# Window attention on one core: staged column heads, two-block stores, nine tiles moved off ScalarE, a new order and a reworked lead

## The chip, the cores and the metric

One core of one Trainium2 chip runs the kernel. The metric is device time in microseconds (us) of one execution. TensorE multiplies matrices into the eight PSUM banks, ScalarE computes exponentials, VectorE and GpSimd do elementwise work, and the SyncE queue issues most transfers. In the profile these are PE (with PEld for its weight loads), ACT, DVE, POOL and SP.

## The reference

The input x is an image of 224 x 224 positions with 96 channels. One product gives q, k and v. The first 48 channels attend inside horizontal stripes, 28 stripes of 8 rows; the other 48 inside vertical stripes, 28 of 8 columns. Each stripe has 1792 tokens. The two results stand side by side and go through the output product.

```python
qkv = jnp.einsum('bhwc,cd->bhwd', x, wqkv)
q, k, v = (qkv[..., :C].copy(), qkv[..., C:2 * C].copy(), qkv[..., 2 * C:].copy())
scale = C2 ** (-0.5)
ah = _softmax(jnp.einsum('bqc,bkc->bqk', qh, kh) * scale, axis=-1)     # horizontal stripes
oh = jnp.einsum('bqk,bkc->bqc', ah, vh).reshape(B, H, W, C2)
av = _softmax(jnp.einsum('bqc,bkc->bqk', qv, kv) * scale, axis=-1)     # vertical stripes
ov = jnp.einsum('bqk,bkc->bqc', av, vv).reshape(B, nw, H, sw, C2)
...
return jnp.einsum('bhwc,cd->bhwd', o, wo)
```

## The kernel before

Two stripes are worked together, one on partitions 0 to 63 and one on 64 to 127. Such a pair is called a block, P = 0 to 27: blocks 0 to 13 are horizontal, 14 to 27 vertical (the first and the second half in what follows). A block has four query chunks (three of 512 columns, one of 256) and 49 score tiles of 128 x 1024 values.

A score tile gets its exponential in one of two ways. An A tile: TensorE multiplies (`qk_fn`, L689) into one of two fixed pairs of PSUM banks, ScalarE takes the exponential (L859). A polynomial tile, kind P or R, leaves ScalarE alone: TensorE multiplies (`s_fn`, L702) into a pair of the four ring banks, VectorE makes a first form of it (L943, and for kind R L945 too), GpSimd squares it (P: L959, L960, L956; R: L956 alone), TensorE multiplies a second time and VectorE finishes (L948). A VectorE pass takes the 1024 columns at once (letters 3 and 4 of the order) or as two halves of 512 (letters 1 and 2). `KINDS` and `KIND_OF` say which tiles of which block are polynomial: nine in a block of kind 1, eight in a block of kind 2. Every tile ends in the product with V (L715, letter v), which gathers in one ring bank; `emit_ot` (L876) takes that out.

Beside the tiles run the fills, letter k: K, Q and V of the next block (L521, L566, brought out on VectorE by L526, L535, L573), and in the second half letter g, the output product of `out_fills` (L637, brought out by L642). Letter f is the last block's own finish, `fin_fills` (L602, L609, L614).

The sequence of TensorE is the string `ORDER`, written out: q is an A tile, 1 and 3 the first multiplication of a polynomial tile, 2 and 4 the second. While it is read, a planner with measured durations (`D_H`, `D_F`, `SEMD`, `XR1` and so on) puts the instructions of the other engines in order; its times set the order alone. Semaphores keep each dependency on the chip. Each engine and queue works strictly in its order, so one late entry holds all that stand behind it.

The array `cat` holds both heads' outputs, 96 channels of every position. `keep_oh` writes horizontal outputs into it, `emit_norm` (L920) vertical ones, `turn_cat` (L414) transposes 96-channel rows to `oc_T` for the output product, which then needs one or two matmuls per 128 tokens as the rows straddle the 128-wide transposes (`wo6` holds six shifted copies of wo). The result goes back into `cat` and out to memory, one DMA per 128 tokens of a stripe (24 KB), from `emit_evict` (issue line L287).

At the start x comes in four loads of 168 KB, two queues with two each, then the weights on SP. `t_lead` transposes x on TensorE (L737), VectorE and ScalarE bring it out and sum it (L749, L753); `KB` makes the mean key out of the sums (L759, L763), the first K goes out by L770. `spin` (L368) puts matmuls on zeros into TensorE's waits, by the planner's times. The first eleven A tiles after the first have their matmuls doubled (`NTWICE`).

Of the kernel before, what the change touches and what calls it, by code (L numbers as in the profile page):

```python
# [20 lines left out]
KINDS = ["PPR PPR PP ", "PPR PRR PPR ", "PPR PPR PR "]  # L21
# [18 lines left out]
NTWICE = 11  # L40


KIND_OF = [0, 1, 1, 1, 1, 1, 1, 1, 1, 1, 1, 1, 1, 1, 2, 2, 2, 2, 2, 2, 2, 2, 2, 2, 2, 2, 2, 2]
ORDER = [
    "kkkqkq3qkq3qkkqkq1qkqq1q3qvkqv2qvkqv2qvqkkvqv1qkvqvkqvv2qvqv1qvvvqvkq2vqvkqkq1qkvvq2qvv2qvvq1vqkvqvvq1vqv2qvkvqvkvq",
    "1vqvvqvq2vvq3qvvvqvv3qqvqvvqkkkq2qvqvkvqv2qkvqv2qkvvvq1qvvvvqvqvv1qvvq2vq2qvkqvvq1vqvkq2vqv2qvvq1qvvqvkqvvkqkvqvkq2vvq2qvv3",
    "qvvqv1qvvq1vqvvqvvqv1qkq1qvvvqvq2qvkkqvqvk2qvvq3qvkqvkvq4qkqv1qvvq4qvkq2vqv1qvq4vqkq2vqv1qvvqvvqv2q1qvvqvkkqq1vkv",
    "qv2qvqv1qvvvqvvqv1qq1vvqvvqvvvq4qvkvq1vqvvqvq2vqv1qvv4qkqvv1qvqvkq2vqkvvq2vkqvkq3vqkqvvvqv1qvq4vqkq3vqkvq4vqvkvq4vqkvq2vk",
    "qvvq1vqvvvvqq2vvvqvvvq2vqvq14qvqkqv3qvkvqvvqvkqv1qkqvvq1vqvkq2vqvkq2qvvvq1qv1qkqvvvqkqvvkq2qvv3qkvqv3qvvqv4qvkqv4qkqvv1",
    "qvqvvvq2vqq1vvqvv1qvvqvqv2qq4vqvkq1vqvvvqvq1vqkvkqkvvq2kqv3qkvqv4qvvqkq1vqvvvqkqvv4qvqkv2qvvq2vqv1qvq4vqvvqkvkvq1qkvvq2v",  # L50
# [5 lines left out]
    "qvvq1vqvvqvq1vqv2qvvq1vqqvvvq1qkvvqvvqkvq4vqkvq1vkqv2qvq3qkvvq2kqvvq2qvv1qvqvvqv2qkvqv3qvkqv4qkqvv1qvvqkkqvkvq2qvvq2vvv",  # L56
    "q3qvvvqvvvqv1qvq2vvvqkq1vqvvq3qvvvqvvqvkq4qkvq1vkqq2vqv4qvkqv2qvvvq1vkqvkq4vqkqv2qvvvq1qvkqvvvq2qkqvvq1vvq2qvvkqkvq1vkq",
    "1qvvqvvq1qvv2qqvvq1vvqvqvv1qvqvqkvqv2qvkqv2qvvqk2qvkqv3qvkvq3qvvvq4qvkvq2qkvqkvq1vqvqkvvqvvq2vqvvq3qvvkq4vqkvqv2qvvq1vk",
    "qvq1vqvvqvvqv1qvv2qvvq1vqq2vqkvq1qvkqvvqvkvqv1qkvvq2qkvvq4vqvvkq1qvvvqvvqkqv4qkvqv4qkvvq1qvvq1vvvqv1qvqvvvvq4qvvvkq2qkvvqkvq2",
    "vvvvqq1vvvvqv2qvvq4vqvkq1qkvkqgqvkgqv3qgvqvqvvgq3qvkvq4qvgqv3qvvkqvvqkqvvgq2vqv2qvvq1vqkqvvvqvq3gqvvq4vqvvkqkq4vqgvvq4qvvkqvq1k",  # L60
    "vqvvqvvq1vqggqgvq1qvgvqkvq4vqgvq2vkqkqvv2qvkqgvq3qvkvqvkqv4qvvqvkq1vqkqv4qvvvqv1qvvqvvqkvqvvq1vqvkkqvq2vvqv4qgvqvvq3qvkvqgvq",
    "gvq1vqvqvvq3vqvkq2vvqv1qvgqvkq4qvkvq4vqvgq4vqvvkq1qvvvqvvqvvkq2qvv1qkvqkvq2qvvgq3qkvqvvqvvvq1qvv2qkqgvqvkqkvqg4qvvqkvvq3vqvgq",
# [111 lines left out]
def bass_standalone__window_attn_cswin__vision_kernel(  # L174
# [28 lines left out]
    with es:  # L203
# [25 lines left out]
        cat = sb("cat", [128, NPH, NPH, 2, C], BF16)  # L229
# [86 lines left out]
        for hf in range(2):  # L316
            for w, q in ((0, "sp"), (1, "actq")):
                dma(q, [], [("x", w, hf)], x0_sb[:, w, hf * FTH:(hf + 1) * FTH, :],
                    x_lead[w][:, hf * FTH * C:(hf + 1) * FTH * C], f"x{w}{hf}", land=3.4 + 1.0 * hf + 0.3 * w)
        dma("sp", [], ["wst"], wst[:, :], wqkv, "w0", land=5.2)  # L320

        pool_now(["iota"], lambda e: e.iota(ident_f[:], [[1, 128]], base=0, channel_multiplier=-1,
                                            allow_small_or_imprecise_dtypes=True), 0.3)
        dve_now(["warm0"], lambda e: e.memset(warm[:, 0:128], 0.0), 0.1)
# [27 lines left out]
        def later():  # L352
# [6 lines left out]
            pool_now([("cat", NPH - 1)], lambda e: e.memset(cat[:, NPH - 1, :, :, C2:C].rearrange("p m w c -> p (m w) c").bitcast(FP32), 0.0), 0.7)  # L359
            pool_now(["wo6z"], lambda e: e.memset(wo6[:].rearrange("p v c -> p (v c)").bitcast(FP32), 0.0), 0.3)  # L360
# [78 lines left out]

        def turn_cat(P, z):  # L440
            b, a = P % 2, P - NPH
            k0, k1 = ((0, 8), (8, NKT))[z]
            flat = cat[:, a, :, :, :].rearrange("p m w c -> p (m w c)")
            x_old = [("x", w) for w in range(2)] if P in (NPH, NP - 1) else []
            turn(f"oc{b}{z}", ["oh", ("cat", a), ("ov", a, z)], [("ocT", b, z), ("catd", a, z)] + x_old,
# [911 lines left out]
```

## Time and profile before

| what | value |
|---|---|
| median of three runs | 1062.24 us (1061.93 to 1062.27) |
| the profiled execution | 1062.68 us, span 1060.9 us |
| granted TensorE clock, mean | 0.999 |
| busy share of the span | PE 97%, DVE 94%, ACT 99%, POOL 88% |
| A tiles (L859) | 1135, 1044.8 us busy |

The span runs from the first to the last instruction; the time of a run holds a little more. A busy share is the union of an engine's instructions. A VectorE instruction that follows another at once starts before that one has ended, so a busy DVE holds less work when packed tightly than the sum of single durations. The views of a stretch are cut at the first A tile of a block: block 1 begins at 47.80 us, block 14 at 526.68, block 15 at 565.17, block 26 at 980.68.

### The profile page before, as it was taken

The page shows a single profiled execution, that of the slowest core. Times are in us where ns is not written, and L with a number is a line of the kernel's source. Part 1 is how long each engine was busy: PE and PEld are TensorE (multiplying, and loading weights), DVE is VectorE, ACT ScalarE, POOL GpSimd, SP SyncE. Part 2 cuts the span into 40 slices and gives each one's busy share as a digit, 9 for nine tenths or more (in the row PEclk, how much of TensorE's full clock was granted, in tenths as well). Part 3 has the DMA queues.
Part 4 walks back from the last instruction along what each step waited for, and adds up shares of the span by engine and source line. Part 5 has one row for each costly group of instructions (what it writes and reads, how often), then busy time and mean ns, then how long its engine had stood idle before and what let it go on. Part 6 is the DMA issues. An engine that isn't in the chain of part 4 may idle for free.

```text
span 1060.9 us, 33547 instructions
## 1 busy us (share of the span) xinstructions
PE 1033.4 (97%) x13812; PEld 393.5 (37%) x13812; DVE 998.2 (94%) x1720; ACT 1049.3 (99%) x1146; POOL 935.5 (88%) x617
## 2 busy tenths in 40 slices
PE   9999999999999999999999999999999999999998
PEld 4333333333333333333334433333343443344433
DVE  8999999999999999999999999999999999999988
ACT  8999999999999999999999999999999999999998
POOL 7999999999988989999999778888888878979784
PEclk9999999999999999999999999999999999999999
DMA  9987648754963874322115334423332342332342
GB/s 182 160 153 112 100 80 145 112 96 84 144 96 56 139 108 69 38 56 58 40 20 99 76 54 76 88 38 77 80 69 52 81 83 49 79 79 40 64 65 44
DMA packets 376217, 88.58 MB, mean 83 GB/s; under 512 B 366944, under 2 KB 373376, under 8 KB 376064
## 3 DMA queue, kind: packets, MB, share of 16 engines
q1 hardware_dynamic: 374816, 85.85, 46.8%
q8 instruction: 108, 1.77, 0.7%
q10 hardware_dynamic: 1120, 0.49, 0.2%
q14 instruction: 45, 0.37, 0.1%
q0 software_dynamic: 128, 0.10, 0.0%
HBM read 28.36 MB, written 28.21 MB: 53 GB/s over the span
## 4 chain that ended last, share of the span: by engine, by line
PE 54%; ACT 28%; DVE 7%; issue 6%; POOL 4%; DMA 0%; ACTq 0%; POOLq 0%; DVEq 0%
ACT PT L859 28%; PE ps L715 20%; PE ps L689 20%; PE ps L702 7%; PE ps L521 3%; DVE qb L943 2%; DVE PT L948 2%; PE ps L637 2%; POOL PT L959 2%; PE ps L566 1%; POOL PT L956 1%; POOL PT L960 1%; DVE PT L945 1%; DVE KT_sb L526 1%; POOL cat L920 0%
## 5 line engine op out<-in xcount | busy, mean ns | idle before, releaser
L859 ACT ACTIVATE PT<-ps 128x1024 bf16<-128x1024 f32 x1135 | 1044.8, 1087 | 2.8 <-PE ps L689 1.8
L689 PE MATMUL ps<-QT_sb,KT_sb 49*64 49x512 bf16 (+1 forms) x5368 | 465.3, 363 | 17.6 <-ACT PT L859 10.5
L956 POOL TENSOR_TENSOR PT<-PT 128x1024 f16<-128x1024 f16 x237 | 445.1, 1892 | 41.1 <-DVE PT L945 24.1
L715 PE MATMUL ps<-PT,V_sb 128*49 128x512 bf16 (+1 forms) x3136 | 464.7, 362 | 0.3
L948 DVE SCALAR_TENSOR_TENSOR PT<-ps,PT 128x512 uint16<-128x512 f32 (+1 forms) x398 | 302.0, 787 | 20.8 <-PE ps L702 13.5
L943 DVE TENSOR_SCALAR qb<-ps 128x512 f16<-128x512 int16 (+1 forms) x404 | 302.3, 778 | 20.3 <-PE ps L702 15.8
L959 POOL TENSOR_TENSOR PT<-qb 128x1024 f16<-128x1024 f16 x141 | 266.1, 1892 | 54.8 <-DVE qb L943 24.9
L689 PEld LDWEIGHTS ps<-QT_sb,KT_sb 49*64 49x64 bf16 x5368 | 136.4, 103 | 305.8 <-ACT PT L859 280.9
L715 PEld LDWEIGHTS ps<-PT,V_sb 128*49 128x49 bf16 x3136 | 134.8, 103 | 211.1 <-issue 181.4
L702 PE MATMUL ps<-QT_sb,KT_sb 53*64 53x512 bf16 (+1 forms) x1896 | 189.4, 389 | 4.0 <-DVE PT L948 0.7
L960 POOL TENSOR_SCALAR PT<-PT 128x1024 f16<-128x1024 f16 x141 | 147.1, 1043 | 12.0
L945 DVE SCALAR_TENSOR_TENSOR PT<-ps,qb 128x512 f16<-128x512 int16 (+1 forms) x166 | 122.5, 766 | 0.5
L702 PEld LDWEIGHTS ps<-QT_sb,KT_sb 53*64 53x64 bf16 (+1 forms) x1896 | 53.8, 104 | 71.2 <-DVE PT L948 21.7
L876 DVE CAST OT_sb<-ps 113x512 bf16<-113x512 f32 x112 | 69.1, 617 | 3.0 <-PE ps L715 2.7
L535 DVE CAST QT_sb<-ps 128x512 bf16<-128x512 f32 (+1 forms) x111 | 67.2, 616 | 2.5 <-PE ps L521 1.7
L526 DVE TENSOR_SCALAR_CACHE_REDUCE KT_sb<-ps 128x512 bf16<-128x512 f32 x108 | 65.4, 616 | 1.3 <-PE ps L521 0.6
L642 DVE CAST cat<-ps 128x480 bf16<-128x480 f32 x84 | 51.5, 617 | 5.1 <-PE ps L637 4.5
L573 DVE CAST V_sb<-ps 128x480 bf16<-128x480 f32 (+1 forms) x84 | 51.7, 620 | 1.5 <-PE ps L566 1.2
L521 PE MATMUL ps<-xT_sb,w_sb 97*64 97x512 bf16 (+1 forms) x224 | 40.7, 364 | 0.0
L521 PE MATMUL ps<-xT_sb,wq_sb 97*64 97x512 bf16 x224 | 40.5, 366 | 0.1
L637 PE MATMUL ps<-wo,oc_all 128*64 128x96 bf16 x1176 | 39.9, 208 | 0.0
L566 PEld LDWEIGHTS ps<-w_sb,xT_sb 96*64 96x64 bf16 x1568 | 33.1, 112 | 17.7 <-issue 7.4
(64 smaller groups left out, 254.7 us busy)
## 6 DMA issues: line engine op xcount, KB each, us to landing
xT_sb<-xt_dram SPq DMA_DIRECT2D x28, 336.0 KB, 4.0
out_dram<-cat SPq DMA_DIRECT2D x382, 24.0 KB, 1.9
xp_dram<-in_x_dram SPq DMA_DIRECT2D x26, 336.0 KB
oc_all<-xp_dram SPq DMA_DIRECT2D x26, 336.0 KB, 4.4
xt_dram<-xT_sb SPq DMA_DIRECT2D x26, 336.0 KB, 6.4
cat<-ohn SPq DMA_DIRECT2D x52, 84.0 KB, 3.2
xt_dram<-xT_sb SPq DMA_DIRECT2D x4, 168.0 KB, 5.3
OT_tr<-OT_sb SPq DMA_TRANSPOSE x40, 3.4
```

The source lines that it names most:

```text
L521: ins = e.matmul(bk[64 * w:64 * w + 64, 0:qs], lhsT=lw, rhs=xT_sb[b][0:C + 1, w, q0:q0 + qs], start=True, stop=True)
L526: return e.tensor_scalar(KT_sb[b][:, q0:q0 + qs], bk[:, 0:qs], alpha, None, ALU.mult, ALU.add, accum_out=ksum[b][:, c:c + 1])
L689: ins = e.matmul(bank(SETS[s] + w)[64 * kh:64 * kh + 64, i * t["qs"]:(i + 1) * t["qs"]], lhsT=KT_sb[b][64 * w:64 * w + CA, kt * 128 + 64 * ...
L702: ins = e.matmul(bank(bp[w])[64 * kh:64 * kh + 64, 0:512], lhsT=KT_sb[b][64 * w:64 * w + nr, kt * 128 + 64 * kh:kt * 128 + 64 * kh + 64], ...
L715: ins = e.matmul(bank(pb)[64 * w:64 * w + CA, 0:t["qs"]], lhsT=V_sb[b][:, w, kt, :], rhs=PT[slot][:, ca:ca + t["qs"]], start=st and i == 0 ...
L859: S.commit("act", 0.0, D_ACT, None, lambda e, s=s, slot=slot: e.activation(PT[slot][:], ps[:, 512 * SETS[s]:512 * SETS[s] + 1024], ACTF.Ex ...
L943: fn, reads, writes = lambda e: e.tensor_scalar(q, l, m, a, ALU.mult, ALU.add), bk, qk
L945: fn, reads, writes = lambda e: e.scalar_tensor_tensor(y.bitcast(FP16), l, -RA * 2.0 ** 16, q, ALU.add, ALU.mult), bk + qk, ptk
L948: fn, reads, writes = lambda e: e.scalar_tensor_tensor(y.bitcast(U16), f, 128.0, y.bitcast(FP16), ALU.mult, ALU.add), bk + ptk, ptk
L956: square = ("pool", D_SQ, lambda e: e.tensor_tensor(y, y, y, ALU.mult), yk + ["pser"], yk)
L959: return [("pool", D_SQ, lambda e: e.tensor_tensor(y, q, q, ALU.mult), qk, yk), ("pool", D_AF, lambda e: e.tensor_scalar(y, y, -(QS * (RB ...
L960: ("pool", D_AF, lambda e: e.tensor_scalar(y, y, -(QS * (RB + RA) / 2) ** 2, 1.0, ALU.add, ALU.mult), yk + ["pser"], yk),
```

## The change

Seven things change together.

1. **Nine tiles.** A new kind 3, "PPR PPR PPR ", has one P tile more than kind 2 and is used for nine of the vertical blocks (15, 16, 17, 19, 20, 21, 23, 24, 25). Nine A tiles become P tiles.
2. **Staged column heads.** `cat` goes. Horizontal outputs lie in `oh_all`; for each vertical block `rows_in` copies its 48 channels into a staging tile `stg` of 128-wide rows (32 of them zero), `emit_norm` writes the vertical 48 beside them, and `turn_cat` transposes whole 128-wide rows. The output product then needs one pair of matmuls per 128 tokens, and one copy of wo. Two new POOL memsets clear `stg` at the start.
3. **Stores of two blocks of 128 tokens.** Results lie in `og`, tokens interleaved by two, and one DMA of 48 KB stores what two of 24 KB did.
4. **Pairs of fills.** A capital K or G in the order makes two fills into two adjacent banks that one VectorE instruction brings out. The order has one K and one G.
5. **Loads of the lead.** The first half of x comes in four quarter loads over both queues, the second in two loads on SP; the weights come on POOL's queue.
6. **Filler.** One spin before the second half of the transposes and one before `KB` are fixed; the two spins after the lead go. The spins in `lead_pe`, by planned times, stay.
7. **Order and planner constants** are new. Block 0 begins `kkqqkkq` in place of `kkkqkq`.

```diff
-KINDS = ["PPR PPR PP ", "PPR PRR PPR ", "PPR PPR PR "]
+KINDS = ["PPR PPR PP ", "PPR PRR PPR ", "PPR PPR PR ", "PPR PPR PPR "]
...
-KIND_OF = [0, 1, 1, 1, 1, 1, 1, 1, 1, 1, 1, 1, 1, 1, 2, 2, 2, 2, 2, 2, 2, 2, 2, 2, 2, 2, 2, 2]
+KIND_OF = [0, 1, 1, 1, 1, 1, 1, 1, 1, 1, 1, 1, 1, 1, 2, 3, 3, 3, 2, 3, 3, 3, 2, 3, 3, 3, 2, 2]
...
-        for hf in range(2):
-            for w, q in ((0, "sp"), (1, "actq")):
-                dma(q, [], [("x", w, hf)], x0_sb[:, w, hf * FTH:(hf + 1) * FTH, :],
...
-        dma("sp", [], ["wst"], wst[:, :], wqkv, "w0", land=5.2)
+        for h2, q in ((0, "sp"), (1, "actq")):
+            for w in range(2):
+                dma(q, [], [("x", w, 0, h2)], x0_sb[:, w, h2 * FQ:(h2 + 1) * FQ, :],
...
+        for w in range(2):
+            dma("sp", [], [("x", w, 1, 0), ("x", w, 1, 1)], x0_sb[:, w, FTH:2 * FTH, :],
...
+        dma("gq", [], ["wst"], wst[:, :], wqkv, "w0", land=4.6)
...
+        pool_now([("stgz", 0)], lambda e: e.memset(stg[0][:, :, :, C:].rearrange("p m w c -> p (m w) c").bitcast(FP32), 0.0), 0.5)
+        pool_now([("stgz", 1)], lambda e: e.memset(stg[1][:, :, :, :].rearrange("p m w c -> p (m w c)").bitcast(FP32), 0.0), 1.8)
...
+        def rows_in(P):
+            b = P % 2
+            dma("sp", ["oh", ("stgz", b)], [("sr", b)], stg[b][:, :, :, 0:C2].rearrange("p m w c -> p (m w) c"),
+                oh_all[:, P - NPH, :, :, :].rearrange("p m w c -> p (m w) c"), f"ri{b}")
...
-            turn(f"oc{b}{z}", ["oh", ("cat", a), ("ov", a, z)], [("ocT", b, z), ("catd", a, z)] + x_old,
+            turn(f"oc{b}{z}", [("sr", b), ("sc", b, z), ("stgz", b)], [("ocT", b, z)] + x_old,
...
-                        for i, (dq_, v) in enumerate(use):
-                            for h in range(2):
-                                ins = e.matmul(bk[64 * h:64 * h + 64, s * C:(s + 1) * C], lhsT=oc_T[b][:, q + dq_, 64 * h:64 * h + 64],
-                                               rhs=wo6[:, v, :], start=i == 0, stop=i == len(use) - 1)
+                        for h in range(2):
+                            ins = e.matmul(bk[64 * h:64 * h + 64, s * C:(s + 1) * C],
+                                           lhsT=oc_T[b][0:C, 4 * (m // 2) + 2 * h + m % 2, :].rearrange("c (t u) -> c u t", u=2)[:, u, :],
+                                           rhs=wo6[0:C, :], start=True, stop=True)
...
+        def spin1():
+            S.commit("pe", 0.0, 0.216, 0.416, lambda e: e.matmul(
+                bank(1)[0:64, 0:512], lhsT=warm[:, 0:64], rhs=warm[:, 0:512], start=True, stop=True),
+                ["warm0", "warm"], [("bank", 1)], tag=("spin",))
...
         for w, hf, bs in ((0, 0, (6, 7)), (1, 0, (2, 3)), (0, 1, (6, 7)), (1, 1, (2, 3))):
+            if (w, hf) == (0, 1):
+                spin1()
...
+        spin1()
         lead_pe(KB, 0)
...
-        spin(S.done[("dve", S.cnt["dve"] - 1)])
-        spin(S.done[("dve", S.cnt["dve"] - 1)], 128)
...
                 if ph_of(P):
-                    tm["sp"] = max(tm["sp"], st) + 1.5
+                    tm["sp"] = max(tm["sp"], st) + (2.2 if P > NPH else 1.5)
+                    if P > NPH:
+                        rows_in(P)
...
-                do_fill(c)
+                do_fill2(c.lower()) if c in "KG" else do_fill(c)
```

More of the change, by code (lines that the diff above doesn't have):

```diff
@@ L59 @@
[L59 to L62, printed above, removed]
@@ L228, in bass_standalone__window_attn_cswin__vision_kernel @@
         OT_sb = [sb(f"OT_sb{i}", [128, NTOK], BF16) for i in range(2)]
-        cat = sb("cat", [128, NPH, NPH, 2, C], BF16)
+        oh_all = sb("oh_all", [128, NPH, NPH, 2, C2], BF16)
+        stg = [sb(f"stg{i}", [128, NKT, 2, 128], BF16) for i in range(2)]
+        og = [sb(f"og{i}", [128, NKT // 2, 2, 2, C], BF16) for i in range(3)]
         OT_tr = [sb(f"OT_tr{i}", [128, NKT, 128], BF16) for i in range(2)]
@@ L883, in emit_evict, with store @@
             if len(st) > 5:
+                store(st, done)
+        def store(st, done):
+            if st:
                 for item in st[5]:
@@ L916, in fn @@
                 if ph_of(P):
[L917 removed]
+                    dst = stg[b][:, k0:k1, :, C2:C].rearrange("p m w c -> p (m w) c")
                 else:
```

215 lines of the change are left out of this document (146 added, 69 removed).

## The prediction, made before the result was known

> **What bounds the kernel now.** I read the busy line first, then the line of ScalarE's exponentials, then the stretches between block starts.
>
> ```profile
> PE 1033.4 (97%) x13812; PEld 393.5 (37%) x13812; DVE 998.2 (94%) x1720; ACT 1049.3 (99%) x1146; POOL 935.5 (88%) x617
> PE 54%; ACT 28%; DVE 7%; issue 6%; POOL 4%; DMA 0%; ACTq 0%; POOLq 0%; DVEq 0%
> ```
>
> Four engines are nearly full, and the chain of waits (second line) names TensorE before ScalarE, so neither line alone decides. The line view of the exponentials does:
>
> ```profile
> L859 ACT ACTIVATE PT<-ps x1135: 1018/1081/1276, 9.6 to 1054.9; 128x1024 bf16<-128x1024 f32 x190
>   PE ps L689: 1.8, 3
>   PEld ps L689: 280.9, 803
> ```
>
> 1135 exponentials start between 9.6 and 1054.9, one each (1054.9 - 9.6) / 1134 = 0.922 us. ScalarE waited for TensorE three times, 1.8 us in all; TensorE's tile loads waited for ScalarE 803 times. TensorE appears in the chain because it hands the banks back and forth with ScalarE, but ScalarE never rests. It is the bound. The question is who takes over when it has fewer tiles.
>
> ```profile
> core 0: us, PE busy (x) PEld busy (x) DVE busy (x) ACT busy (x) POOL busy (x), PEclk, DMA share, GB/s
> 47.80:526.68 478.88, 465.82 (x5828) 167.43 (x5824) 461.08 (x774) 478.32 (x522) 446.00 (x293) 1.00 0.58 94
> 565.17:980.68 415.51, 409.88 (x5854) 163.77 (x5850) 389.05 (x643) 415.16 (x451) 355.29 (x222) 1.00 0.35 70
> 980.68:1055.97 75.29, 74.20 (x1062) 29.52 (x1058) 67.44 (x138) 75.29 (x83) 54.86 (x37) 1.00 0.34 57
> 1055.97:1060.90 4.93, 0.69 (x12) 0.28 (x12) 2.30 (x12) 0.00 (x1) 0.68 (x2) 0.77 0.33 65
> ```
>
> First row: blocks 1 to 13, nine polynomial tiles each; DVE is busy 96.3%, POOL 93.1%, and ACT still 99.9%. So a DVE busy at 96% does not stop ScalarE. Second row: blocks 15 to 25, eight polynomial tiles and the output product each; DVE 93.6%, POOL 85.5%. All nine moved tiles fall there. The last row is the tail, 4.93 us without exponentials.
>
> **The change part by part.** *Nine tiles off ScalarE.* 9 x 0.922 = 8.3 us less, as ScalarE is the bound from 9.6 us on. What it costs elsewhere, from the line view with shapes apart:
>
> ```profile
> L943 DVE TENSOR_SCALAR qb<-ps 128x512 f16<-128x512 int16 x334 | 216.9, 684 | 12.2 <-PE ps L702 8.8
> L943 DVE TENSOR_SCALAR qb<-ps 128x1024 f16<-128x1024 int16 x70 | 85.5, 1222 | 8.1 <-PE ps L702 6.9
> L948 DVE SCALAR_TENSOR_TENSOR PT<-ps,PT 128x1024 uint16<-128x1024 f32 x76 | 92.9, 1222 | 6.0 <-PE ps L702 3.6 <-POOL PT L956 0.9 <-DVE V_sb L573 0.3
> L956 POOL TENSOR_TENSOR PT<-PT 128x1024 f16<-128x1024 f16 x237 | 445.1, 1892 | 41.1 <-DVE PT L945 24.1 <-DVE wq_sb L552 7.5 <-PE ps L715 0.7
> L959 POOL TENSOR_TENSOR PT<-qb 128x1024 f16<-128x1024 f16 x141 | 266.1, 1892 | 54.8 <-DVE qb L943 24.9 <-ACT PT L859 8.9 <-PE ps L702 7.2
> L960 POOL TENSOR_SCALAR PT<-PT 128x1024 f16<-128x1024 f16 x141 | 147.1, 1043 | 12.0
> L637 PE MATMUL ps<-wo,oc_all 128*64 128x96 bf16 x1176 | 39.9, 208 | 0.0
> 699.86 1.29 DVE L943 TENSOR_SCALAR qb<-ps 128x512 f16<-128x512 int16 x2
> 1041.93 0.46 PE L637 MATMUL ps<-wo,oc_all 128*64 128x96 bf16 x14
> ```
>
> A P tile is two DVE passes and three POOL passes. POOL: 1.892 + 1.043 + 1.892 = 4.83 us, nine times 43.4. The blocks 15 to 25 would then hold 355.3 + 43.4 = 398.7 in 415.5 - 8.3 = 407.2 us, 98%. That is more than the 93.1% of blocks 1 to 13, but a late POOL delays only finishing passes, which the order may put off by many tiles, and blocks 14, 26 and 27 have room (54.86 of 75.29 in the last two). I take 0 for POOL and leave its risk in the stall term below. DVE: a pass of 1024 columns lasts 1.222, two halves 1.29 (the row of two at 699.86, which shows the second starting 1.29 - 0.684 = 0.61 after the first). Two passes: 2.4 to 2.6 us a tile, 22 to 23 us in all. 389 + 22 = 411 in 407 us would be over full. But busy time counts the last 0.08 us of each pass as work (0.684 long, next start after 0.61); 643 instructions x 0.08 = 51 us of these 389 vanish at most when one follows another at once. As some follow at once already, I take about a third of it, 17 us: some 372 + 9 x 2.35 = 393 in 407, 96.5%. The same correction leaves blocks 1 to 13 at about 461 - 774 x 0.08 / 3 = 440 of 479, 92%. So DVE has a slack of some 14 us in 407 and is fuller than any stretch this trace shows.
>
> *Stalls of the denser blocks.* This is the unknown. From below it is 0: the stretch at 92% made ScalarE wait almost nothing. From above: every added pass exposed, 9 x 2.44 = 22 us, as if each moved tile stopped TensorE's order and so ScalarE for its full two passes. The trace lies near the lower end, as 92% cost next to nothing, but 96.5% leaves half the slack; I take 0.2 us for each of the 11 blocks that hold the tiles, together +2.3, and keep 0 to +7 for the range.
>
> *TensorE.* Every moved tile has two multiplications in place of one, 0.22 us more (four matmuls more in a tile raise 0.41 to 0.63 in the rows of the lead below), 2 us in all. The output product falls from 1176 to 784 matmuls: 14 take 0.46 with 0.21 of it the last one's latency, so 0.02 each, 392 x 0.02 = 8 us less. TensorE is relieved on balance, and it waits for ScalarE now; worth 0 by itself. A strided weight load in the new product, if it costs double, is at most 784 x 0.02 = 16 us more in 1050 and is hidden in waits of 280.9; from below nothing too. I take 0.
>
> *Staging and stores, on SP's queue.*
>
> ```profile
> out_dram<-cat SPq DMA_DIRECT2D x382, 24.0 KB, 1.9
> cat<-ohn SPq DMA_DIRECT2D x52, 84.0 KB, 3.2
> xT_sb<-xt_dram SPq DMA_DIRECT2D x28, 336.0 KB, 4.0
> oc_all<-cat SPq DMA_TRANSPOSE x28, 3.7
> 707.94 10.24 SPq L287 DMA_DIRECT2D out_dram<-cat  x10
> 718.27 1.47 SPq L414 DMA_TRANSPOSE oc_all<-cat  x1
> 719.79 1.33 SPq L287 DMA_DIRECT2D xT_sb<-xt_dram  x2
> 721.16 3.12 SPq L287 DMA_DIRECT2D out_dram<-cat  x5
> ```
>
> Half of some 390 stores go, at about 0.62 us of issue each when queued (five in 3.1 us): 120 us of SP's time, 8.7 a block. Added per vertical block: one `rows_in` (0.7 us of issue like the other block copies, landing like 336 KB, about 4 us) and two transposes a third longer, 3.7 to some 4.5. The transpose at 718.27 stood behind ten stores; now it stands behind five, so it starts earlier than it grows. `rows_in` goes out at a block's first tile, while its transposes come when that block's products with V are done, tens of us later; what waits for `rows_in` on SP (loads of the next block's x, stores) is held only if the older transpose of the same buffer is late. Hidden, 0; with the cover gone, a late g holds TensorE, a rival below. POOL's two clears of `stg` (about 2.3 us by the clear of 448 columns in 0.47) stand before its first square at 12.81, in an idle of 3.29; 0. The pairs K and G save under 0.1 us each of DVE.
>
> *The lead.*
>
> ```profile
> 0.74 0.89 SPq L287 DMA_DIRECT2D cat<-in_x_dram  x2
> 3.04 0.47 POOL L342 MEMSET oc_all<- 128x448 f32 x1
> 3.99 3.22 PE L737 MATMUL ps<-ident,cat 112*96 112x112 bf16 x32 [0.33 <-DMA cat<-in_x_dram]
> 5.41 0.34 POOL L344 COPY w_sb<-wst 96x192 bf16<-96x192 bf16 x1 [0.85 <-DMA wst<-in_wqkv_dram]
> 7.25 0.54 ACT L753 ACTIVATE xT_sb<-ps 96x448 bf16<-96x448 bf16 x1
> 8.21 0.38 PE L368 MATMUL ps<-warm 128*64 128x512 bf16 x1
> 8.38 2.58 DVE L770 TENSOR_SCALAR KT_sb<-ps,kb_sb 128x128 bf16<-128x128 f32 x5
> 9.11 0.41 PE L689 MATMUL ps<-QT_sb,KT_sb 49*64 49x512 bf16 x4
> 9.88 0.63 PE L689 MATMUL ps<-QT_sb,KT_sb 49*64 49x512 bf16 x8
> 12.81 3.74 POOL L959 TENSOR_TENSOR PT<-qb 128x1024 f16<-128x1024 f16 x2 [3.29 <-DVE qb L943]
> ```
>
> x lands at 3.99, 3.2 us after its issue; quarters may land 0.3 to 0.4 sooner. The 32 transposes are back to back, 0.10 each, so they gain that; the fixed spin in their midst gives back up to 0.43 (512 columns at 0.9 ns, the rate of 112 in 0.10), unless TensorE waits there anyway. The last transposes are brought out at 7.25 and the first K at 8.38, yet the first tile's matmuls start at 9.11, behind the spins of 8.21 and three K fills. With no spins after `KB` and two fills in place of three, about 0.3 of this goes. The weights come earlier on POOL's queue or at least not later than 7.1, where Q needs them. Between -0.8 and +0.5 I take -0.3.
>
> *The tail.*
>
> ```profile
> 1052.88 3.10 ACT L859 ACTIVATE PT<-ps 128x1024 bf16<-128x1024 f32 x3
> 1057.47 0.99 DVE L614 SCALAR_TENSOR_TENSOR cat<-ps,rc,cat 128x96 bf16<-128x96 f32 x4
> 1058.53 0.53 POOL L287 DMA_DIRECT2D out_dram<-cat  x1 [2.41 <-DVE cat L614]
> ```
>
> The exponentials end at 1055.98, the last finish at 1058.46, its store lands at the end. The arithmetic stays; fewer stores can spare half an issue. Between -0.5 and +0.3 I take -0.2.
>
> The sum, against the profiled execution: 1060.9 - 8.3 + 2.3 - 0.3 - 0.2 = 1054.4 of span; that run took 1062.68, 1.8 more than its span, and the median of the runs is 0.4 below it: 1054.4 + 1.8 - 0.4 = 1055.8.
>
> **The rivals.**
>
> *VectorE becomes the bound in blocks 15 to 25.* If the tails of 0.08 us do not pack away, these blocks last as long as DVE's 411 us, plus what it cannot avoid waiting: today 415.5 - 389 = 26, of which a fourth would already give 418. Then the nine tiles bring nothing and only lead and tail are left: about 1061, from 1059 to 1063. For it speaks the count of four ring banks, of which a second pass takes two; against it that blocks 1 to 13 run at 96.3% busy without a stall.
>
> *A later clock.* The transposes run at 0.9 ns a column, the tiles at 0.43 (0.22 for 512): half rate in the lead. Should half rate last over the first three tiles, as the spins after `KB` are gone, their doubled matmuls take 0.87 in place of 0.44 and a fill 0.43 in place of 0.22, some 0.6 us above what ScalarE hides in each: +1.8, 1057.6. [...]
>
> *Late transposes: slower than before.* The g letters stand at fixed places. If `rows_in` and longer transposes bring `oc_T` later than planned, a g stops TensorE, and ScalarE with it once its two bank pairs are used up (about 0.9 us). There are two transposes a block, 26 in all; from (1064.4 - 1055.8) / 26 = 0.33 us exposed on each it decides; at 0.5 each, 1055.8 + 13 = 1069. Against it: SP is freed of 8.7 us a block, and no wait of the output product for a DMA shows today (L637 idle 0.0).
>
> **How the numbers follow.** This kernel tells 0.2%, 2.1 us, from no change. ScalarE stays the bound: 0.70 (1053 to 1059.5), of which the low stall is likeliest. VectorE binds: 0.14, half of it faster by over 2.1 us and half within. Later clock alone: 0.05, faster. Late transposes: 0.11, nearly all slower. Faster 0.70 + 0.07 + 0.05 = 0.82, same 0.08, slower 0.10. The range takes in a stall of nothing with the best lead (1055.8 - 2.3 - 0.5 = 1053.0) and VectorE as bound to its middle, 1061.5.
>
> **What would show it.** 1126 exponentials at 0.92 to 0.925 us from start to start, the first at about 9.3, and ScalarE over 99% busy in blocks 15 to 25, with DVE 97% or more. Wrong: intervals of 0.94 and more there with the tile loads waiting for DVE (VectorE binds), idle of L637 or its loads ended by a DMA (late transposes), first tiles over 1 us apart (clock).

## The result: slower by 1.2%

| | before | after |
|---|---|---|
| median | 1062.26 us (1061.93 to 1063.39, 6 runs) | 1075.30 us (1071.58 to 1077.22, 6 runs) |
| ratio to before | | 1.0117, 95% interval 1.0094 to 1.0139 |
| profiled execution | 1062.68, span 1060.9 | 1076.99, span 1075.2 |
| exponentials: count, first start, last end | 1135, 9.57, 1055.97 | 1126, 9.08, 1068.66 |

The prediction said 1055.8, 1053.0 to 1061.5: wrong in size and in sign. Where a time below can't be read without it, the run's mean granted clock stands beside it: it is about 0.999 in a run that keeps the full clock, and lower in one that runs a stretch at half clock (0.989 in the profiled run after).

Three rows of the page after: the granted clock in 40 slices (9 is full, 5 is half), and the groups of the exponentials and of the tiles' weight loads (busy us, mean ns, then idle time ahead and what ended most of it).

```profile
PEclk9999999999999999999999599999999999999999
L879 ACT ACTIVATE PT<-ps 128x1024 bf16<-128x1024 f32 x1126 | 1039.6, 1077 | 20.9 <-PE ps L703 19.3
L703 PEld LDWEIGHTS ps<-QT_sb,KT_sb 49*64 49x64 bf16 x5332 | 136.6, 104 | 303.2 <-ACT PT L879 271.4
```

Before, ScalarE waited 1.8 us for TensorE in the whole run; now 19.3. The clock row shows one slice at half. The stretches tell where (blocks 1 to 13; block 15; the half clock inside it; blocks 16 to 25; 26 and 27; the tail):

```profile
core 0: us, PE busy (x) PEld busy (x) DVE busy (x) ACT busy (x) POOL busy (x), PEclk, DMA share, GB/s
46.82:526.16 479.34, 466.49 (x5830) 166.35 (x5824) 461.44 (x773) 478.52 (x521) 448.04 (x294) 1.00 0.50 93
564.99:619.00 54.01, 44.27 (x522) 16.38 (x522) 37.28 (x67) 38.05 (x42) 37.56 (x24) 0.78 0.64 79
589.80:613.70 23.90, 19.22 (x192) 6.57 (x192) 14.86 (x25) 11.55 (x12) 15.51 (x10) 0.50 0.37 60
619.00:992.60 373.60, 365.00 (x5002) 141.70 (x4996) 360.81 (x614) 371.47 (x403) 346.11 (x216) 1.00 0.51 86
992.60:1068.66 76.06, 75.00 (x1014) 29.64 (x1012) 72.78 (x134) 75.78 (x83) 66.73 (x45) 1.00 0.39 67
1068.66:1075.20 6.54, 1.75 (x32) 1.00 (x30) 3.61 (x19) 0.00 (x0) 3.07 (x6) 0.95 0.26 77
```

Blocks 1 to 13 last what they did (479.34 and 478.88). Block 15 lasts 54.01; its 40 exponentials at 0.917 us each, about the pace of blocks without a wait (block 4 after: 36.69 us for 40), would take 36.68, so 17.33 are lost there. Losses of other blocks and runs below are counted in the same way. Blocks 16 to 25 with eight of the nine tiles gone take 373.60, against 377.83 before (from its block starts at 602.85 and 980.68): 4.2 gained of 8 x 0.917 = 7.3. The tail is 6.54 against 4.93. So one block holds nearly the whole result: 1060.9 - 0.49 (lead) + 16.33 (block 15, against 37.68 before) - 3.46 (all blocks after it) + 0.31 (the blocks ahead of it) + 1.61 (tail) = 1075.2.

The waits of the whole run (sum, times, longest; the longest of each lies in block 15), and the timeline of block 15:

```profile
DVE rn L963 <- DMA OT_tr<-OT_sb: 11.1, 3, 9.2
PE ps L650 <- DVE PT L1003: 9.2, 1, 9.2
ACT PT L879 <- PE ps L703: 19.3, 20, 9.9
```

```profile
592.46 0.23 DVE L963 RECIPROCAL rn<-OT_tr 128x12 f32<-128x12 bf16 x1 [9.24 <-DMA OT_tr<-OT_sb]
594.48 0.61 PE L650 MATMUL ps<-wo,oc_all 96*64 96x96 bf16 x10 [9.16 <-DVE PT L1003]
596.57 1.94 ACT L879 ACTIVATE PT<-ps 128x1024 bf16<-128x1024 f32 x2 [9.88 <-PE ps L703]
```

VectorE stood 9.24 us at a reciprocal of 0.23 us (`rn`, first step of `emit_norm`): the transpose of block 14's second half (`turn_ot`) had not landed. VectorE's passes queued behind it, so TensorE stood 9.16 and ScalarE 9.88. From 589.8 on the clock is at half for 23.9 us. The stall took some 10 us of the 17.3, which leaves 7.3 for the half clock; an experiment below tests this split. Why the transpose was late shows in the SyncE queue (issue time, length), first before, then after:

```profile
560.29 4.99 SPq L414 DMA_TRANSPOSE oc_all<-cat  x2
565.33 1.35 SPq L414 DMA_TRANSPOSE OT_tr<-OT_sb  x1
566.72 1.05 SPq L287 DMA_DIRECT2D xT_sb<-xt_dram  x2
567.87 1.24 SPq L414 DMA_TRANSPOSE OT_tr<-OT_sb  x1
```

```profile
564.21 3.20 SPq L292 DMA_DIRECT2D stg<-oh_all  x2
570.53 8.99 SPq L424 DMA_TRANSPOSE oc_all<-stg  x2
581.79 0.60 SPq L292 DMA_DIRECT2D stg<-oh_all  x1
582.43 4.08 SPq L292 DMA_DIRECT2D xT_sb<-xt_dram  x2
586.62 1.24 SPq L424 DMA_TRANSPOSE OT_tr<-OT_sb  x1
```

The wanted transpose is the last row of each: 567.87 before, 586.62 after. The output product of block 27's horizontal channels is queued ahead of all others, so its `rows_in` and two `turn_cat` stand at the passage from block 14 to 15. Now the first `turn_cat` waits for the copy (to 570.53), the second for the first (the planner's list of dependencies still has both overwrite an old x), the next copy for the second, and the wanted transpose stands behind them all.

### The profile page after: what moved, and what is told of

The parts are those of the page before. It is cut to its first block, busy times and chain, and to the rows that moved or that the text cites. A ratio compares the mean times of both kernels' runs of the same rounds, so it can differ in the third digit from the quotient of the medians.

```text
span 1075.2 us, 32746 instructions
## 1 busy us (share of the span) xinstructions
PE 1035.2 (96%) x13454; PEld 387.7 (36%) x13454; DVE 1015.0 (94%) x1749; ACT 1044.0 (97%) x1137; POOL 982.7 (91%) x651
## 4 chain that ended last, share of the span: by engine, by line
PE 48%; ACT 19%; DVE 12%; POOL 12%; issue 6%; DMA 3%; SPq 0%; ACTq 0%; POOLq 0%; DVEq 0%
ACT PT L879 18%; PE ps L729 18%; PE ps L703 17%; PE ps L716 7%; POOL PT L1014 5%; DVE PT L1006 4%; POOL PT L1017 3%; DVE qb L1001 3%; PE ps L536 3%; POOL PT L1018 2%; DVE PT L1003 2%; PE ps L581 2%; DMA OT_tr<-OT_sb 1%; PE ps L650 1%; DMA oc_all<-stg 1%
## 5 line engine op out<-in xcount | busy, mean ns | idle before, releaser
L879 ACT ACTIVATE PT<-ps 128x1024 bf16<-128x1024 f32 x1126 | 1039.6, 1077 | 20.9 <-PE ps L703 19.3
L1014 POOL TENSOR_TENSOR PT<-PT 128x1024 f16<-128x1024 f16 x246 | 461.7, 1892 | 25.5 <-DVE PT L1003 16.5
L1006 DVE SCALAR_TENSOR_TENSOR PT<-ps,PT 128x512 uint16<-128x512 f32 (+1 forms) x409 | 312.7, 793 | 16.8 <-PE ps L716 7.4
L1001 DVE TENSOR_SCALAR qb<-ps 128x512 f16<-128x512 int16 (+1 forms) x421 | 313.4, 776 | 14.8 <-PE ps L716 10.1
L1017 POOL TENSOR_TENSOR PT<-qb 128x1024 f16<-128x1024 f16 x150 | 283.1, 1893 | 31.9 <-DVE qb L1001 19.3
L716 PE MATMUL ps<-QT_sb,KT_sb 50*64 50x512 bf16 (+1 forms) x1968 | 198.5, 393 | 7.1 <-DVE PT L1006 1.4
L716 PEld LDWEIGHTS ps<-QT_sb,KT_sb 50*64 50x64 bf16 (+1 forms) x1968 | 56.0, 104 | 82.6 <-DVE PT L1006 26.3
L656 DVE CAST og<-ps 128x480 bf16<-128x480 f32 x82 | 50.1, 615 | 3.2 <-PE ps L650 2.3
L978 POOL TENSOR_TENSOR stg<-OT_tr,rn 128x768 bf16<-128x768 bf16 (+1 forms) x26 | 34.1, 1313 | 11.4 <-DVE rn L963 8.9
L650 PE MATMUL ps<-wo,oc_all 96*64 96x96 bf16 x784 | 31.9, 211 | 10.0 <-DVE PT L1003 9.2
L536 PE MATMUL ps<-xT_sb,w_sb 97*64 97x512 bf16 x224 | 40.5, 365 | 0.5 <-DVE qb L1001 0.2
```

Of the source, the lines that this page charges most:

```text
L536: ins = e.matmul(bk[64 * w:64 * w + 64, 0:qs], lhsT=lw, rhs=xT_sb[b][0:C + 1, w, q0:q0 + qs], start=True, stop=True)
L716: ins = e.matmul(bank(bp[w])[64 * kh:64 * kh + 64, 0:512], lhsT=KT_sb[b][64 * w:64 * w + nr, kt * 128 + 64 * kh:kt * 128 + 64 * kh + 64], ...
L879: S.commit("act", 0.0, D_ACT, None, lambda e, s=s, slot=slot: e.activation(PT[slot][:], ps[:, 512 * SETS[s]:512 * SETS[s] + 1024], ACTF.Ex ...
L1001: fn, reads, writes = lambda e: e.tensor_scalar(q, l, m, a, ALU.mult, ALU.add), bk, qk
L1006: fn, reads, writes = lambda e: e.scalar_tensor_tensor(y.bitcast(U16), f, 128.0, y.bitcast(FP16), ALU.mult, ALU.add), bk + ptk, ptk
L1014: square = ("pool", D_SQ, lambda e: e.tensor_tensor(y, y, y, ALU.mult), yk + ["pser"], yk)
```

## The experiments

**One transpose moved.**

```diff
 # SyncE queue, block 14 to 15
-turn_cat(27,1); rows_in(15); x(17) x2; turn_ot(14,1)
+turn_ot(14,1); turn_cat(27,1); rows_in(15); x(17) x2
```

> The changed kernel with one entry of SP's queue moved: the transpose of block 14's second half of outputs (OT_tr) goes ahead of the second transpose of block 27's staged rows. Theory 1, the queue: that transpose starts near 574 in place of 586.6, lands before VectorE comes to the reciprocal that reads it (583), VectorE's wait of 9.2 us there falls under 1 us, TensorE never stops long enough to lose its clock, and the time is 1077 - 17 = 1060 us, from 1057 to 1063. Theory 2, the density of the nine tiles on VectorE and GpSimd: the time stays at 1072 to 1077.

1066.56 us (1063.63 to 1068.18), ratio 1.0035 (1.0023 to 1.0046): two thirds of the loss is gone, and the 9.24 with it. In its place the next transpose, OT(15,0), stands behind `turn_cat(14,1)`: VectorE waits 3.3 at most and TensorE 3.28, and the four matmuls right behind that gap take 0.64 us in place of 0.41 (mean clock of the run 0.993). The wait that was aimed at is gone as forecast, but the time is above the 1057 to 1063 expected: one late entry hid another. From its waits (sum, times, longest):

```profile
DVE rn L967 <- DMA OT_tr<-OT_sb: 4.7, 4, 3.3
```

**One false wait removed.** `turn_cat(27,1)` no longer waits for `turn_cat(27,0)`: the old x does not lie in that buffer after the change.

```diff
-x_old = [("x", w) for w in range(2)] if P in (NPH, NP - 1) else []
+x_old = [("x", w) for w in range(2)] if P == NPH else []
```

> The changed kernel without the dependency of block 27's two transposes on the old x tile (their target no longer overlaps it), so the second does not wait for the first to land. A smaller dose of the same: the chain ahead of block 14's transpose becomes some 4 us shorter. Theory 1, the queue: VectorE's wait of 9.2 us falls to 4 to 6 us, and the time to 1063 to 1071 us, the lower end if the clock stays up. Theory 2, the density: no change, 1072 to 1077.

1071.10 us (1068.07 to 1074.15), ratio 1.0082 (1.0053 to 1.0111). The transpose goes out 4 us sooner, at 582.5; VectorE's longest wait is 6.2, where 4 to 6 was expected, and ScalarE waits 7.2 at most. The median lies between two pairs of runs, 1068 at clock 0.995 and 1074 at 0.988 and 0.989. Only a part of the loss is gone: the copy that the first `turn_cat` waits for, and the loads, still stand ahead.

**The stand-still filled.** 36 matmuls on zeros in TensorE's order where it stood.

```diff
+if g[:2] == ("G", NP - 1) and g[3] == 20:
+    for _ in range(36):
+        spin1()
```

> The changed kernel with 36 matmuls of 512 columns on zeros (7.8 us at full clock) put ahead of the output product at which TensorE stands still at 585. Theory 1: the standstill stays at 9.9 us for ScalarE, but TensorE's clock stays at full rate, so about 7 us of the 17 go: 1068 to 1071 us. Rival: the 24 us at half clock are hidden behind ScalarE and all the loss is the standstill: 1075 to 1078 us.

1068.96 us (1068.26 to 1070.72), ratio 1.0064 (1.0049 to 1.0079), mean clock 0.998 in all four runs. Its timeline at the wait, and the stretch around it in the view of stretches:

```profile
585.82 7.96 PE L816 MATMUL ps<-warm 128*64 128x512 bf16 x36 [1.42 <-ACT PT L879]
591.53 0.23 DVE L963 RECIPROCAL rn<-OT_tr 128x12 f32<-128x12 bf16 x1 [9.35 <-DMA OT_tr<-OT_sb]
```

```profile
564.00:612.50 48.50, 46.38 (x586) 19.24 (x582) 38.58 (x70) 39.11 (x44) 37.73 (x24) 1.00 0.72 92
```

VectorE still waits 9.35, but TensorE is busy and the clock of the stretch stays at 1.00. Block 15 loses 9.6 us in place of 17.3, so the half clock alone was worth 7 to 8 of them. TensorE's idle time brings it here, not the late data.

**The old tiles with the new staging.** Lead, staging and stores of the change, with `KIND_OF` and `ORDER` of before.

```diff
-KIND_OF = [0, 1, ..., 2, 3, 3, 3, 2, 3, 3, 3, 2, 3, 3, 3, 2, 2]
+KIND_OF = [0, 1, ..., 2, 2, 2, 2, 2, 2, 2, 2, 2, 2, 2, 2, 2, 2]
 # and ORDER of before
```

> The changed kernel's lead, staging and stores, with the tile kinds and the order of the kernel before (eight polynomial tiles in each vertical block, no pairs of fills). Theory 1, the queue: the copy into the staging tile and the chain behind it are late at block 15 with any tiles, a standstill of 5 to 15 us there and 1065 to 1080 us. Theory 2, the density: without the nine tiles nothing stalls, 1060 to 1062 us.

1082.82 us (1076.32 to 1092.09), ratio 1.0199 (1.0143 to 1.0255). The stall is there without a single moved tile: two waits of VectorE of 3.6 and 4.7 us in block 15, half rate from the first of them on (ten matmuls of the output product take 0.61 us at 581.14 and 0.40 at 575.82; mean clock of the run 0.984), and 18.0 us lost in the block. The nine tiles are not its cause; the lead, the staging and the stores were changed together here and not told apart. The tail is 5.08, close to the 4.93 of before, so the longer tail comes from the new order and not from the stores of 48 KB. From its waits:

```profile
DVE rn L963 <- DMA OT_tr<-OT_sb: 10.6, 7, 4.7
```

**The queue in the order of its data.** The changed kernel without the false wait, and its SyncE queue at this passage permuted; no other engine's order moves.

```diff
+turn_ot(14,1) ahead of turn_cat(27,0), turn_cat(27,1)
+rows_in(14), x(17) x2 behind them, turn_cat(14,0) ahead of rows_in(15)
```

> The changed kernel with the SyncE queue of the passage from block 14 to 15 put in the order in which the data come: the copy for block 27, then the transpose of OT (14,1), then the two transposes of block 27 (the second no longer waiting for the first), the copy for block 14, the two loads of x, and each transpose of block 14 before what is needed later. Nothing is added or left out, all other engines keep their order. Theory 1 (the queue's order makes the stall, and the half clock follows from the stall): no wait of 3 us or more of VectorE for OT_tr, no stretch of half clock, the 17.3 us of block 15 gone: 1058.5 to 1061. Rival (the denser blocks themselves, or the copies' load on the DMA engines, stall it whatever the order): 5 us or more stay in blocks 15 to 27, 1064 to 1070.

Nine of twelve runs at 1059.68 to 1061.40, all with clock 0.999 or 1.0; three at 1069.85 to 1074.39 with 0.983 to 0.992. Median 1060.80, ratio 1.0008 (0.9978 to 1.0038): in most runs the loss is gone, and no gain over the kernel before is shown. The three are not what theory 1 expected, and none of them was traced. In the profiled run (1060.26) VectorE's longest wait for `OT_tr` is 1.1 us, and block 15 (564.91 to 601.82) loses 0.23 us in place of 17.33. The SyncE queue in its timeline:

```profile
564.22 0.62 SPq L292 DMA_DIRECT2D stg<-oh_all  x1
567.69 1.23 SPq L424 DMA_TRANSPOSE OT_tr<-OT_sb  x1
570.21 3.90 SPq L424 DMA_TRANSPOSE oc_all<-stg  x2
```

and a stretch of 37.63 us around block 15 in the view of stretches, ScalarE busy 37.55 of 37.63 us, VectorE 36.95, DMA share 0.97:

```profile
564.73:602.36 37.63, 37.34 (x530) 14.84 (x526) 36.95 (x69) 37.55 (x42) 36.81 (x24) 1.00 0.97 114
```

With the same nine tiles and the same copies, neither VectorE at 98% nor the busy DMA engines stall ScalarE here. The rival falls for this block.

**The same with the old tiles.** The same order of the queue, into which `turn_ot(14,0)` had to be fitted too, with `KIND_OF` and `ORDER` of before.

> The same order of the queue, with the tiles and the string ORDER of before: lead, staging and stores of two blocks of 128 tokens alone, without the nine tiles. Its unmended run had 18.0 us in block 15. Theory 1: these go, 1062 to 1065, since staging and stores then give and take nothing and the rest of its small stalls (some 2 us) stays. Against the other run of this call it gives what the nine tiles are worth once the stall is gone: by my prediction 6 us (8.3 less 2.3), by the blocks of the changed kernel 4 or 5 (small stalls of 4, a tail of 1.5 from the new order). Rival (the nine tiles are worth nothing, VectorE binds): both equal.

1067.25 us median (1065.10 to 1079.20), ratio 1.0058 (1.0032 to 1.0084); the profiled run 1066.12 at clock 1.0, 5.9 us above the 1060.26 of the run with the nine tiles. That is 9 x 0.917 = 8.3 less 1.5 of tail, 0.6 of small stalls and 0.3 of lead: tiles and order together are worth about the 6 that I gave the tiles, but by luck, as I had 2.3 of stalls and nothing of tail in it. The run with the old tiles is slower than I expected, by 2 us in the median, and 3.4 slower in span than the kernel before: lead, staging and stores together cost something even with the large stall gone. VectorE waits for `OT_tr` five times, 3.7 us (before: never), and all its blocks together lose 9.6 us against 5.6 before.

**The tail.** Beside the mended queue, output products (g) come earlier in the last block and the last products with V ahead of finishes.

```diff
-...q4vqgvq4vqgvqvv1qfqvvvqvvfqv4qvqg2qvfqfvvfqvvqvgqvvgvffvvvfvfff
+...q4vqgvq4vqggvqvv1qfqvvvqvvfqv4qgvqg2qvfqfvvfqvvqvqvvvffvvvvffff
```

> As the first run of this call, and in the last block four output products (g) come earlier, two products with V ahead of two finishes. Theory (the tail of 6.55 us in place of 4.93 comes from late work on VectorE after the last exponential, as the new order has it): tail 5.2 to 6.0, 0.5 to 1.3 us less than the first run. Rival (the stores of 48 KB make the longer tail): tail stays at 6.5.

1064.44 us (1062.56 to 1066.67), ratio 1.0016 (1.0008 to 1.0025). The tail fell as expected, to 5.89. But all eleven runs have a clock of 0.996 to 0.998, and the trace of one shows a reason: a moved g came 2 us ahead of its transpose. The timeline of TensorE in the profiled run, and its stretch at half clock:

```profile
1040.75 0.41 PE L658 MATMUL ps<-wo,oc_all 96*64 96x96 bf16 x10
1043.34 0.61 PE L658 MATMUL ps<-wo,oc_all 96*64 96x96 bf16 x10 [2.18 <-DMA oc_all<-stg]
```

```profile
1042.80:1049.60 6.80, 6.26 (x48) 2.06 (x50) 4.12 (x8) 2.96 (x3) 2.04 (x2) 0.50 0.21 53
```

TensorE idle for 2.18 us, 6.8 us at half clock, 6.0 us lost in block 27: the miss is mine, and a small copy of the large one. The other ten runs were not traced.

**The lead without its filler.** The mended queue, and the two fixed `spin1` of the lead left out.

```diff
-if (w, hf) == (0, 1):
-    spin1()
...
-spin1()
 lead_pe(KB, 0)
```

> As the first run of this call, without the two fixed fillers of the lead (the planner then puts one of 128 columns where the second stood). If they bring the full clock earlier: first exponential 0.3 to 0.8 us later than in the first run, clock granted at 7 us or later. If they only take time: first exponential 0.2 to 0.4 sooner. In no run did the clock of the lead come later than the 7.3 us of before, so my rival of a later clock gives no more than 1 us either way.

Seven of twelve runs at 1059.77 to 1063.27, three at 1066.90 to 1069.73 with a mean clock as high as the others' (0.999 in the traced one in spite of what follows: the view of stretches gives 1.00 for 9.77 to 34.60 too), and two at 1069.23 and 1073.81 with 0.990; median 1062.24, ratio 1.0017 (0.9991 to 1.0043). My "no more than 1 us" was wrong. In the profiled run (1069.73) the first exponential is at 9.77, and TensorE runs at the slow rate until 34.6. Two rows of its timeline, then one of the mended queue with filler (start, us, count at the end):

```profile
22.84 0.64 PE L711 MATMUL ps<-QT_sb,KT_sb 49*64 49x512 bf16 x4
34.63 0.41 PE L711 MATMUL ps<-QT_sb,KT_sb 49*64 49x512 bf16 x4
```

```profile
20.41 0.41 PE L711 MATMUL ps<-QT_sb,KT_sb 49*64 49x512 bf16 x4
```

Four matmuls take 0.64 in place of 0.41, and block 0 loses 8.7 us in place of 0.04. With the filler, four traces show full rate from 4.93 us on in the earliest (the filler's matmul of 512 columns takes 0.40 there) and from 7.16 on in the latest (two matmuls in 0.41), and the first exponential at 8.58 to 9.43. The late full rate is seen in this one trace, and the seven low times show that it does not come in every run without the filler. In 38 runs with the filler (the mended queue alone, and the three versions after this one) none took 1066 us or more at a clock of 0.999.

**The tail again.** The pair `gg` put back, two g one tile earlier.

```diff
-...qvqg2qvfqfvvfqvvqvgqvvgvffvvvfvfff
+...qvqg2qvfqgfvvfqvvqgvqvvvffvvvvffff
```

> The mended queue, and in the tail two output products one A tile earlier each and two products with V ahead of two finishes; the pair of output products that stood for a transpose in the trial before goes back to its place. Theory 1 (a wait of TensorE of some 2 us for a transpose brought the half clock there; the tail is late work on VectorE): no wait of L658 for a DMA, no half clock in block 27, tail 5.8 to 6.0: 0.6 to 0.8 us less than the mended queue alone, 1059 to 1060.5 in most runs. Rival (the order of the tail itself disturbs the clock): half clock again near the end, 1062 or more.

Nine of twelve runs at 1059.40 to 1061.15, three at 1066.28 to 1082.30 with clock 0.974 to 0.991; median 1060.61, ratio 0.9990 (0.9972 to 1.0008). No wait of L658 for a DMA and no half clock in block 27; the tail is 6.13, 0.5 less than the 6.61 of the mended queue, where 0.6 to 0.8 less was expected. Block 27 gives 0.5 back as small stalls (0.67 lost in place of 0.22), and the spans are equal (1058.4 and 1058.5): this order of the tail brings nothing. Three of twelve runs with a lower clock are as many as in the mended queue alone.

**One more transpose, and two more.** With the queue and the tail of the run above, first OT(15,0) is moved, then the two others.

```diff
-turn_cat(14,1); turn_ot(15,0)
+turn_ot(15,0); turn_cat(14,1)
 # the second version also:
-turn_cat(15,0); turn_ot(15,1)
+turn_ot(15,1); turn_cat(15,0)
-rows_in(19); x(21) x2; stores; turn_ot(18,1)
+turn_ot(18,1); rows_in(19); x(21); stores; x(21)
```

> As the other run of this call, and the first transpose of OT of block 15 ahead of the second transpose of block 14, behind which it stood. In the mended queue alone 3 of 12 runs were at 1069.9 to 1074.4 with a mean clock of 0.983 to 0.992, the others at 1059.7 to 1061.4. Theory 1 (what is left of VectorE's wait there, some 1 us, sometimes brings the half clock): the wait goes, and so do the runs above 1065. Rival (the half clock comes from elsewhere, or the second transpose of block 14 is now late for its product): 2 or more of 12 runs again above 1065, or a wait of L658 for a DMA.

Seven of nine runs at 1059.78 to 1060.68, one at 1066.46, and the profiled one at 1077.93, which caught the half clock; ratio 0.9982 (0.9968 to 0.9996). So two runs above 1065 are left: theory 1 fails as it was put, and the rival that the half clock comes from elsewhere holds. Its timeline (queue, VectorE, TensorE), then the stretch at half clock, then the same stretch in the version before it, undisturbed:

```profile
606.84 4.28 SPq L424 DMA_TRANSPOSE oc_all<-stg  x1
611.22 1.23 SPq L424 DMA_TRANSPOSE OT_tr<-OT_sb  x1
615.20 0.23 DVE L971 RECIPROCAL rn<-OT_tr 128x12 f32<-128x12 bf16 x1 [1.50 <-DMA OT_tr<-OT_sb]
616.55 0.41 PE L724 MATMUL ps<-QT_sb,KT_sb 53*64 53x512 bf16 x4 [1.16 <-DVE og L664]
```

```profile
618.40:662.80 44.40, 44.09 (x378) 13.54 (x376) 27.38 (x42) 29.40 (x29) 28.86 (x19) 0.50 0.43 70
```

```profile
618.40:662.80 44.40, 43.88 (x592) 16.86 (x592) 43.41 (x74) 43.80 (x49) 42.15 (x28) 1.00 0.56 91
```

The place is the next one in the queue: OT(15,1) stands behind a `turn_cat` whose issue takes 4.28. VectorE waits 1.50, TensorE 1.16, and then 378 matmuls are done in 44.40 us in place of 592. In the undisturbed version the same wait was 0.95 and TensorE's gap 0.66. Hence the last run, which moves that transpose too:

> As the run with the transpose of OT of block 15 moved, and two more moved: the second one of block 15 ahead of the first transpose of block 15's rows (behind which it held VectorE for 1.50 us, TensorE for 1.16, with 44.4 us of half clock right after it), and the second one of block 18 ahead of the copy and the loads of the next blocks (VectorE waited 1.0 for it). Theory 1 (waits of some 1 us and more on the queue's order are what sets the clock back): VectorE's waits for OT_tr under 0.5 us each, no run above 1063, all at 1058.5 to 1060.5. Rival (the half clock comes by chance, or from another place): one run in five still at 1066 or more, as in the three versions before it.

1058.68 us (1058.39 to 1059.41, five runs, all at clock 0.999 or 1.0), ratio 0.9964 (0.9951 to 0.9978): 0.36% faster than the kernel before, and faster than the changed kernel. Its waits for `OT_tr`, and its exponentials on the page:

```profile
DVE rn L971 <- DMA OT_tr<-OT_sb: 0.4, 1, 0.4
```

```profile
L887 ACT ACTIVATE PT<-ps 128x1024 bf16<-128x1024 f32 x1126 | 1038.5, 1079 | 4.9 <-PE ps L711 3.2
```

VectorE waits 0.4 in all, ScalarE 3.2 for TensorE. That no run was disturbed fits theory 1, but with about one in four disturbed in the three versions with a mended queue and undisturbed lead before it, five clean runs would come by luck one time in four; that these short waits were the only trigger is not shown. One trace speaks against a gap of TensorE of this size as a sufficient cause: in the lead without filler a gap of 1.30 us, longer than the 1.16, was not followed by half clock (mean clock of the run 0.999).

```profile
739.63 0.40 PE L737 MATMUL ps<-PT,V_sb 128*49 128x512 bf16 x2 [1.30 <-DVE PT L1011]
```

## Why the prediction was wrong

**The step that failed is "Staging and stores, on SP's queue ... Hidden, 0".** I counted SyncE's time (120 us of issue saved) and let a saving in sum stand for a queue that is on time. The costs arise at one passage, where block 27's rows are brought in and turned between two blocks; I wrote that transposes come "tens of us later" than their copies, which holds for a block's own rows and not for these. In an ordered queue the price is that of the most urgent entry behind a wait: 9.24 us at VectorE, plus some 7 of half clock. I asked who stands behind each added wait for stores and loads of x, and not for `turn_ot`, whose rows before (565.33 and 567.87) lay in the trace. The copy itself was too cheap as well: I gave it about 4 us to land, and the page after has 6.2 (median):

```profile
stg<-oh_all SPq DMA_DIRECT2D x15, 336.0 KB, 6.2
```

**Late transposes** was my rival at 0.11, with the right queue and the wrong victim: I watched `oc_T` and L637, spread over 26 transposes at 0.33 each. What came late was `OT_tr`, at one place, and VectorE stood there, not the output product. L650's idle of 9.2 ends by VectorE, not by a DMA; by my own list of signs the rival would not have been recognised.

**Nine tiles, -8.3:** right as a count: 1126 exponentials at the same pace. Net, 5.9 us lie between the two runs of the mended queue with new and old tiles, which differ in the order as well.

**Stalls of the denser blocks, +2.3 (0 to 7):** all blocks together lose 9.8 us in the last version against 5.6 before, so +4.2: inside the bounds, nearly twice my value, which also counted 11 blocks where nine hold the tiles (0.2 x 11 is 2.2, 0.2 x 9 is 1.8). How much of the 4.2 belongs to the tiles and how much to the staging is not settled: with the old tiles and the new staging the loss was 9.6, though there with 3.7 us of waits for `OT_tr` in it.

**VectorE becomes the bound:** fell. In blocks 16 to 25 after, ScalarE is busy 371.47 of 373.60, and VectorE at 96.6%.

**TensorE, 0:** held: a weight load of the new product takes 111 ns (110 before), and with the queue mended ScalarE waits 3.2 us for it in the whole run.

**Lead, -0.3:** -0.5 in the profiled run, between -0.1 and -1.0 in the others with the filler, as x lands 0.7 sooner (the first transposes start at 3.27 in place of 3.99). **Later clock:** in the changed kernel it doesn't happen, but it can be far dearer than my 1.8: in the trace without the filler the half rate went on for 24.8 us after the first exponential and cost 8.7, where I had put three tiles.

**Tail, -0.2:** +1.6. I looked at stores and not at what the new order leaves for after the last exponential: VectorE is busy 3.61 us there in place of 2.30, and with the old order the tail is 5.08.

With the queue mended the median comes out 2.9 above mine (1058.7 and 1055.8). In span, where the parts can be added, it is 3.2 (1057.6 and 1054.4): 1.9 of stalls and 1.4 of tail, less 0.1 in the lead.

## What to carry to other kernels

Where a change puts a dependent chain (copy, transpose, next copy) into an ordered queue, list what stands behind each of its waits at the busiest passage, with the time that each entry's data are ready: the price is the lateness of the most urgent one, whatever the queue saves in sum. Put urgent short transfers ahead of long chains, and look for the next late one when the first is mended. Where TensorE is as busy as here (97% before), price a gap of 2 us and more as the gap plus a stretch at half clock (here 6.8 us of it with a gap of 2.18, 23.9 with one of 9.16), and count a gap of 1.1 to 1.5 us as a risk of one (here one of four).

## What the runs showed of the hardware

Gaps of TensorE in mid-kernel far shorter than 9 us came with half clock. Of 2 us and more, these did: 2.18 us (6.8 us at clock 0.50), 3.15 (ten matmuls in 0.61 us in place of 0.40), 3.28 (four in 0.64 in place of 0.41) and 9.16 (23.9 us at 0.50); one of 6.3, where the false wait was removed, lies in a run with a mean clock of 0.995. With 36 matmuls on zeros in the place of the 9.16, VectorE waited 9.35 and the clock of the stretch stayed at 1.00. Of four gaps of 1.1 to 1.5 us one was followed by half clock (1.16), and three were not (1.11, 1.30 and 1.42); what else decides there is open. The stretches at clock 0.50 in the views above lasted 6.8, 23.9 and 44.4 us, the last though TensorE was busy for 44.09 of it. Half rate cost 0.3 to 0.4 us for each us: 7.3 of 23.9 (by the split above), 17.7 of 44.4 (span 1076.1 against 1058.4 in the version before it), 8.7 of 24.8 in the lead without its filler. What decides the end of such a stretch stays open.

The issue of a `turn_cat` holds the queue for 1.4 to 4.3 us after the change (22 rows that hold a single one, median 1.9), against 1.3 to 2.5 before (24 rows, median 1.4). The long ones in the rows above (3.90 for two, 4.28 for one) come 6 and 4 us after a copy into `stg` was issued; whether the issue waits for such transfers was not tested.
